# Decode attention and a small FFN on one core: FFN and output projection by column tiles, one product for the softmax denominators, unused matmuls in a loop

## The chip, the cores and the metric

The kernel runs on one core of one Trainium2 chip. The metric is device time in microseconds (us) of one execution, and several executions are compared by their median.

## What is computed

Two tokens (a batch of 2, one query each, width 512) pass a layer norm. The result feeds an attention block with a cache of 8192 keys and values for each of 32 heads of 128, and beside it a two-layer FFN of width 1792 with a ReLU. Both results are added to the input:

```python
xn = _layernorm(x)
q = (xn @ wq) by heads                       # 2 x 32 heads x 128
p = softmax(q . k_cache * 128 ** -0.5)       # over 8192 keys
o = p . v_cache
out = x + o.reshape(2, 4096) @ wo + relu(xn @ w1) @ w2
```

All inputs and the output are bf16. The key and value caches are 128 MiB each; wq and wo are 4 MiB each, w1 and w2 1.75 MiB each. Each byte is read once.

## The kernel before, in words

**The loop.** There are 64 pairs of batch and head. A turn of the loop takes U = 4 of them, so there are NP = 16 turns. Partition p of the tile `ks` (8 MiB) holds 256 keys of one pair, 32 partitions to a pair; `vs` holds the values in the same way. There is one buffer each for keys and for values. In a turn TensorE transposes the 256 key blocks (line 275), while VectorE and ScalarE copy the results to the 32 tiles `kT` (line 429). TensorE then multiplies them with the queries into the PSUM tile `Sc` (line 282). VectorE takes maxima (476, 483), ScalarE takes exponentials (550), adding up each pair's sum into `RS`, one partition slice to a pair, and TensorE multiplies the weights with the values (335). At the end of a turn, in all but the last two, TensorE does `WARM` = 24 products of the identity with itself into `ms`, which nobody reads (346).

**Loads.** All large loads stand in SyncE's queue in program order (lines 182 to 196). The keys of turn t+1 are issued when the transposes of turn t are done, the values of turn t+1 when the value products of turn t are done. After the transposes of the last turn, SyncE issues w1, w2 and then wo in four pieces of 18, 8, 4 and 2 of its 32 rows j (`cuts`, line 153; a row is 128 partitions by 512 columns). They go into `ks`, in front of the output store that waits for `osb`.

**After the loop**, in TensorE's order: four fp32 products of `RS` with `onesh`, one to a pair slot, give the denominators in `Sc` (line 356); four products put x into the eight columns `fin` of `Sc` (362); 56 products of w1 blocks with the two columns of xn give the hidden layer in `ms` (373). Meanwhile VectorE turns denominators and value sums into the normalised output `OTn` (494 to 512), and takes the ReLU to `hT` (516). TensorE transposes `OTn` (385) and regroups it with four products by `sel` (389), and VectorE makes `OX` of it (522). Then come 56 products with w2 and 128 with wo (line 400, in `project`). In these the weights are the stationary operand, 128x128 each, and the two tokens the moving one, two columns wide. All add into `fin`. Before each piece of wo TensorE waits for its load. Last come a copy to `yT` (526), a transpose (420), a copy to `osb` (528) and the store (196).

GpSimd sets up the identity, `sel`, `onesh` and zeros (213 to 230), and in the loop copies the queries of a turn (236).

Of the kernel before, what the change touches and what calls it, by code (L numbers as in the profile page):

```python
# [15 lines left out]
LAG = 32  # L16
TR = (21, 25)
BC = 32
WARM = 24
ON_ACT = (0, 3, 5)  # L20


# [1 line left out]
def kernel(  # L24
# [35 lines left out]
    QG = H * Dh // 512  # L60
    QH = 512 // Dh
    Z = (QG - 1) * Bsz

    inv_sqrt = float(Dh) ** -0.5
    eps = 1e-5
# [9 lines left out]
    def sem(name):  # L75
        return tc.alloc_semaphore(name)
# [10 lines left out]
    kT = [sb([P, EG, P], bf16, f"kT{i}") for i in range(NG)]  # L87
    identb = sb([P, P], bf16, "identb")
    sel = sb([H, DQ, P], bf16, "sel")
    onesh = sb([P, U, P], f32, "onesh")  # L90
    onesb = sb([1, P], bf16, "onesb")
    eps_t = sb([P, 1], f32, "eps_t")
    xsb = sb([Bsz, D], bf16, "xsb")
# [3 lines left out]
    rinv = sb([Bsz, 1], f32, "rinv")  # L97
    xn = sb([Bsz, KT, P], bf16, "xn")

    xz = sb([P, KT, 2 * Z + Bsz], bf16, "xz")  # L100
    qs = sb([QG * Bsz, 512], bf16, "qs")
    qb = sb([P, N], bf16, "qb")
    q4 = sb([P, U], bf16, "q4")
# [2 lines left out]
    mcol = sb([P, 2], bf16, "mcol")  # L106
    mx = sb([1, 2, U], bf16, "mx")
    nm = sb([P, 2, U], f32, "nm")
    RS = sb([P, 2, NP], f32, "RS")
    NM = sb([P, 2, N], f32, "NM")  # L110
    OTf = sb([P, 2, N], f32, "OTf")
    lo = sb([P, N], f32, "lo")
# [6 lines left out]
    OG = sb([P, 2, N], f32, "OG")  # L119
    OTn = sb([P, Bsz, H], bf16, "OTn")  # L120
    Ob = sb([H, Bsz, Dh], bf16, "Ob")
    OX = sb([P, WJ, Bsz], bf16, "OX")
    hT = sb([P, FJ, Bsz], bf16, "hT")
    yT = sb([P, Bsz, KT], bf16, "yT")
    osb = sb([Bsz * KT, P], bf16, "osb")

# [23 lines left out]
    K_all = A_k_cache.rearrange("b h (m kk) d -> (b h m) (kk d)", kk=KB)  # L150
    V_all = A_v_cache.rearrange("b h (m kk) d -> (b h m) (kk d)", kk=KB)
    wo_v = A_wo.rearrange("(p j) n -> p j n", j=WJ)
    cuts = (0, 18, 26, 30, WJ)
    NC = len(cuts) - 1

    KSPLIT = (0, NP - 1)
    VSPLIT = (1, NP - 1)
    NL = 16 * NP
    piece = [(dX, 32), (dQ, 32)] + [(sem(f"dWo{c}"), 16) for c in range(2, NC)]
    qp = ot[0:QG * Bsz, :]  # L160
    tpq = ms[:, 0:N // 2].bitcast(bf16).rearrange("p (l c) -> p l c", l=QH)
    tpx = tp[0][:].rearrange("p g k -> p (g k)")[:, 0:KT * Bsz].rearrange(
        "p (kt b) -> p kt b", b=Bsz
    )
    hp = ms[:, 128:128 + FJ * Bsz].rearrange("p (j b) -> p j b", b=Bsz)
    ox = ms[:, 256:256 + Bsz * WJ]
    fin = Sc[:, 512:512 + KT * Bsz]

# [42 lines left out]
    @(lambda f: f(nc.gpsimd))  # L211
    def _(g):
        g.memset(identb[:], 0.0).then_inc(sG, 1)
        g.memset(sel[:], 0.0).then_inc(sG, 1)
        g.memset(onesh[:], 0.0).then_inc(sG, 1)
        g.wait_ge(sG, 1)
        g.affine_select(
            out=identb[:], in_=identb[:], compare_op=ALU.not_equal, fill=1.0,
            base=0, pattern=[[-1, P]], channel_multiplier=1,
        ).then_inc(sI, 1)  # L220
        g.wait_ge(sG, 2)
        g.affine_select(
            out=sel[:], in_=sel[:], compare_op=ALU.not_equal, fill=1.0,
            base=0, pattern=[[-1, DQ], [1, P]], channel_multiplier=-DQ,
        ).then_inc(sI, 1)
        g.wait_ge(sI, 2)
        g.memset(prm[:], 0.0).then_inc(sG, 1)
        g.wait_ge(sG, 4)
        for u in range(U):
            g.memset(onesh[u * HP:(u + 1) * HP, u, :], 1.0).then_inc(sI, 1)  # L230
            g.wait_ge(sI, 3 + u)
        g.wait_ge(sV, 100)
        for t in range(NP):
            if t > 0:
                g.wait_ge(sS, 2 * t)
            g.tensor_copy(q4[:], qb[:, U * t:U * t + U]).then_inc(sQ1, 1)  # L236
            for d, split in ((dK, KSPLIT), (dV, VSPLIT)):
                if t not in split:
                    g.wait_ge(d[0], 16 * (t + 1)).then_inc(d[1], 16)
        g.wait_ge(dO, 16).then_inc(sG, 1)  # L240


    @(lambda f: f(nc.tensor))
    def _(pe):
# [53 lines left out]
        def spread(i):  # L298
# [2 lines left out]
                bc[:, i, :], lhsT=onesb[:], rhs=mx[:, i, :], start=True, stop=True  # L301
            ).then_inc(sB, 1)

        regs = counters(pe, mybir.EngineType.PE)
        reg, g, h = regs[0], regs[1:3], regs[3:]
        with pe.Fori(16, NL + 1, 16) as n16:
# [35 lines left out]
                if first == KB // 2 - 1:  # L342
                    t.then_inc(sW, 1)
            with pe.If_lt(reg, NP - 1):
                for i in range(WARM):
                    pe.matmul(  # L346
                        ms[:], lhsT=identb[:],
                        rhs=identb[:].rearrange("p (o k) -> p o k", o=1).to_broadcast([P, 4, P]),
                        start=True, stop=True,
                    )  # L350
            advance(pe, regs)

        pe.wait_ge(sI, 2 + U)
        dbp = Sc[:, 0:2 * N].rearrange("p (t u) -> p t u", u=U)
        for u in range(U):
            t = pe.matmul(
                dbp[:, :, u], lhsT=onesh[:, u, :], rhs=RS[:].rearrange("p i t -> p (i t)"),
                start=True, stop=True,
            )
        t.then_inc(sH, 1)  # L360
        for k in range(KT):
            pe.matmul(
                fin[:, k * Bsz:(k + 1) * Bsz],
                lhsT=xsb[:, k * P:(k + 1) * P],
                rhs=identb[0:Bsz, 0:Bsz],
                start=(k == 0),
                stop=False,
            )
        pe.wait_ge(dW1, 16)
        w1_v = w1_sb.rearrange("p kt (f j) -> p kt j f", j=FJ)  # L370
        for j in range(FJ):
            for kt in range(KT):
                i = pe.matmul(
                    hp[:, j, :],
                    lhsT=w1_v[:, kt, j, :],
                    rhs=xz[:, kt, Z:Z + Bsz],
                    start=(kt == 0),
                    stop=(kt == KT - 1),
                )
        i.then_inc(sF, 1)  # L380

        pe.wait_ge(sV, 108)
        tO = tp[0][0:H, 0:Bsz, :]
        for b in range(Bsz):
# [10 lines left out]
            )  # L395
        t.then_inc(sH, 1)

        def project(w, j, x, last=False):
            for k in range(KT):
                t = pe.matmul(  # L400
                    fin[:, k * Bsz:(k + 1) * Bsz],
                    lhsT=w[:, j, k * P:(k + 1) * P],
                    rhs=x[:, j, :],
                    start=False,
                    stop=(last and k == KT - 1),
                )
            return t

        pe.wait_ge(sF, 2)
        pe.wait_ge(dW2, 16)  # L410
        for j in range(FJ):
            project(w2_sb, j, hT)
        pe.wait_ge(sV, 110)
        for c in range(NC):
            pe.wait_ge(*piece[c])
            for j in range(cuts[c], cuts[c + 1]):
                t = project(wo_sb, j, OX, j == WJ - 1)
        t.then_inc(sH, 1)
        pe.wait_ge(sV, 111)
        pe.transpose(  # L420
            tp[1][0:Bsz * KT, 0, :], yT[:].rearrange("p b c -> p (b c)"), identb[:]
        ).then_inc(sH, 1)

    def kcopies(eng, act, h):
# [8 lines left out]
    def _(v):  # L433
        v.memset(eps_t[:], eps).then_inc(sV, 1)
        v.memset(onesb[:], 1.0)
        v.memset(xz[:], 0.0).then_inc(sZ, 1)
        v.wait_ge(dX, 16)
        v.bn_stats(out=stats[:], in_=xsb[:]).then_inc(sV, 1)
        v.wait_ge(sV, 2)
# [50 lines left out]
        def both(ap):  # L490
# [21 lines left out]
        v.tensor_tensor(  # L512
            out=OTn[:].rearrange("p b h -> p (b h)"), in0=OG[:, 0, :], in1=OG[:, 1, :], op=ALU.add
        ).then_inc(sV, 1)
        v.wait_ge(sF, 1)
        v.tensor_scalar(
            out=hT[:], in0=hp, scalar1=0.0, scalar2=None, op0=ALU.max,
        ).then_inc(sF, 1)
        v.wait_ge(sH, 2)
        v.tensor_copy(Ob[:], tp[0][0:H, 0:Bsz, :]).then_inc(sV, 1)  # L520
        v.wait_ge(sH, 3)
        v.tensor_copy(
            OX[:], ox.rearrange("p (b j) -> p j b", b=Bsz)
        ).then_inc(sV, 1)
        v.wait_ge(sH, 4)
        v.tensor_copy(yT[:], fin.rearrange("p (c b) -> p b c", c=KT)).then_inc(sV, 1)
        v.wait_ge(sH, 5)
        v.tensor_copy(osb[:], tp[1][0:Bsz * KT, 0, :]).then_inc(sE, 1)


    @(lambda f: f(nc.scalar))
    def _(a):
        a.wait_ge(sV, 3)
        a.activation(
            out=rstd[:], in_=mv[:, 1:2], func=ACTF.Sqrt, bias=eps_t[:Bsz], scale=1.0
        ).then_inc(sA, 1)

        a.copy(nm[:, 0, 0:1], eps_t[:]).then_inc(sO, 1)
        regs = counters(a, mybir.EngineType.Activation)
        reg, g, h = regs[0], regs[1:3], regs[3:]  # L540
        with a.Fori(0, NP) as t:
            kcopies(a, True, h)
            for i in range(2):
                a.wait_ge(sB, g[i])
                a.copy(nm[:, i, :], bc[:, i, :]).then_inc(sN, 1)  # L545
                a.wait_ge(sN, g[i])
                for u in range(U):
                    own = slice(u * HP, (u + 1) * HP)
                    k = slice(i * KB // 2, (i + 1) * KB // 2)
                    x = a.activation(  # L550
                        out=prm[own, k, u],
                        in_=S[own, k, u],
                        func=ACTF.Exp,
                        bias=nm[own, i, u:u + 1],
                        scale=1.0,
                        accum_out=RS[own, i, bass.ds(t, 1)],
                    )
                x.then_inc(sP, 1)
            a.copy(NM[:, :, bass.ds(t * U, U)], nm[:]).then_inc(sC, 1)
            a.wait_ge(sW, g[1])  # L560
            a.copy(OTf[:, :, bass.ds(t * U, U)], oh[:, :, 0:U]).then_inc(sO, 1)  # L561
            advance(a, regs)
        a.wait_ge(sV, 102)
        a.activation(out=F[:], in_=df[:], func=ACTF.Exp, scale=1.0).then_inc(sA, 1)
# [1 line left out]
_INS = ['A_x', 'A_k_cache', 'A_v_cache', 'A_wq', 'A_wo', 'B_x', 'B_w1', 'B_w2']  # L566
_OUTS = [((2, 1, 512), 'bfloat16')]
# [25 lines left out]
```

## Time and profile before

| What | Value |
|---|---|
| Median of 6 runs | 659.55 us (658.26 to 662.0) |
| Profiled execution, device time | 659.12 us |
| Its span, first to last instruction | 657.3 us |
| Mean granted TensorE clock | 0.967 |
| Read from HBM | 280.50 MB, 427 GB/s over the span |
| Loop's last value product ends | 642.61 us into the span |
| Output store issued | 654.88 us into the span |

The profile counts times from the start of the span. For each engine it tells when instructions ran, what it waited for, and which instruction or load ended the wait. PE is TensorE's products, PEld its loads of stationary operands, DVE is VectorE, ACT is ScalarE, POOL is GpSimd, SP is SyncE. SPq is an engine's queue issuing. A DMA row in a chain is the time from a load's issue to its landing. PEclk is the clock that TensorE was granted, as a share of full speed.

### The profile page before, as it was taken

The numbers are of one execution on the slowest core, as the hardware profiler recorded it, in microseconds if no ns is written. First come the engines' busy times: TensorE is split into PE (matmuls) and PEld (weight loads), VectorE is DVE, ScalarE is ACT, GpSimd is POOL, SyncE is SP. The second block draws the span as 40 slices with busy tenths as digits, with TensorE's granted clock in tenths as the row PEclk, the third lists the DMA queues.
The fourth block names the chain that finished last, engine by engine and source line by source line (L and its number), as shares of the span: only waits on it lengthen the run. The fifth ranks groups of instructions, "written<-read, shape, count | busy, mean of one in ns | idle before, by whom it ended". The sixth has DMA issues, their size and how long they took to land.

```text
span 657.3 us, 27600 instructions
## 1 busy us (share of the span) xinstructions
PE 600.3 (91%) x12987; PEld 544.7 (83%) x12987; DVE 261.9 (40%) x503; ACT 290.8 (44%) x532; POOL 7.1 (1%) x30
## 2 busy tenths in 40 slices
PE   2786999999999999999999999998999999999997
PEld 0586887978889798888979878896987879798987
DVE  1440450716235071632507154260715417072721
ACT  1332443636345263543537354343725435372730
POOL 2000000000000000000000000000000000000000
PEclk9986999999899899999989999999999999899997
DMA  9999999999999999999999999999999999999997
GB/s 379 448 441 437 396 423 443 423 443 419 435 443 431 439 415 423 447 447 431 423 427 443 447 431 423 423 447 443 435 411 435 447 443 431 411 439 427 429 421 290
DMA packets 6223, 280.66 MB, mean 427 GB/s; under 512 B 706, under 2 KB 708, under 8 KB 964
## 3 DMA queue, kind: packets, MB, share of 16 engines
q1 hardware_dynamic: 6208, 280.50, 99.0%
q8 instruction: 8, 0.13, 0.1%
q14 instruction: 3, 0.02, 0.0%
q10 hardware_dynamic: 4, 0.00, 0.0%
HBM read 280.50 MB, written 0.00 MB: 427 GB/s over the span
## 4 chain that ended last, share of the span: by engine, by line
PE 61%; DMA 35%; DVE 1%; issue 1%; SPq 0%; ACT 0%; ACTq 0%
PE tp L275 34%; DMA ks<-in_A_k_cache_dram 31%; PE ot L335 11%; PE Sc L282 10%; PE ms L346 6%; DMA ks<-in_A_wo_dram 4%; DVE mcol L476 1%; PE ms L294 0%; PE ms L300 0%; SPq L194 0%; ACT L429 0%; ACT kT L429 0%; SPq L191 0%; SPq L182 0%; SPq L170 0%
## 5 line engine op out<-in xcount | busy, mean ns | idle before, releaser
L429 DVE COPY kT<-tp 128x1024 bf16<-128x1024 bf16 x320 | 209.3, 688 | 248.8 <-PE tp L275 243.2
L275 PEld LDWEIGHTS tp<-identb,ks 128*128 128x128 bf16 x4096 | 230.6, 98 | 18.3 <-DMA ks<-in_A_k_cache_dram 16.4
L275 PE MATMUL tp<-identb,ks 128*128 128x128 bf16 x4096 | 233.1, 220 | 12.6 <-DMA ks<-in_A_k_cache_dram 11.7
L429 ACT COPY kT<-tp 128x1024 bf16<-128x1024 bf16 x192 | 188.1, 1014 | 122.7 <-PE tp L275 122.7
L335 PE MATMUL ot<-prm,vs 128*128 128x64 bf16 x4096 | 139.2, 197 | 1.6 <-issue 1.6
L335 PEld LDWEIGHTS ot<-prm,vs 128*128 128x128 bf16 x4096 | 135.1, 100 | 3.5 <-issue 1.7
L282 PE MATMUL Sc<-q,kT 128*128 128x64 bf16 (+8 forms) x4096 | 134.2, 192 | 3.2 <-issue 3.1
L282 PEld LDWEIGHTS Sc<-q,kT 128*128 128x128 bf16 x4096 | 129.6, 98 | 4.7 <-issue 3.4
L346 PE MATMUL ms<-identb 128*128 128x512 bf16 x336 | 74.8, 379 | 0.0
L476 DVE TENSOR_REDUCE mcol<-Sc 32x1 bf16<-32x128 f32 x128 | 37.1, 290 | 93.6 <-PE Sc L282 92.3
L550 ACT ACTIVATE prm<-Sc,nm 32x128 bf16<-32x128 f32 x128 | 69.0, 539 | 5.4
L545 ACT COPY nm<-ms 128x4 f32<-128x4 f32 x32 | 5.2, 163 | 142.1 <-PE ms L300 142.1
L346 PEld LDWEIGHTS ms<-identb 128*128 128x128 bf16 x336 | 31.8, 97 | 36.4
L561 ACT COPY OTf<-ot 128x8 f32 x16 | 2.7, 166 | 76.2 <-PE ot L335 76.2
L550 ACT ACTIVATION_READ_ACCUMULATOR prm<-Sc,nm x128 | 32.1, 251 | 0.0
L294 PE MATMUL ms<-identb,mcol 128*1 128x128 bf16 x32 | 7.0, 218 | 22.1 <-DVE mcol L476 22.1
L294 PEld LDWEIGHTS ms<-identb,mcol 128*1 128x1 bf16 x32 | 2.5, 79 | 23.9 <-issue 23.1
L429 ACT ACT_TABLE_LOAD x16 | 20.5, 1283 | 3.6 <-issue 3.5
L254 PE MATMUL ot<-vs,xz 128*16 128x512 bf16 x32 | 8.5, 431 | 8.7 <-DMA vs<-in_A_wq_dram 8.7
L483 DVE TENSOR_REDUCE mx<-ms 1x4 bf16<-1x128 bf16 x32 | 8.9, 279 | 13.8 <-PE ms L294 13.8
L254 PEld LDWEIGHTS ot<-vs,xz 128*16 128x16 bf16 x32 | 3.1, 98 | 13.7 <-issue 10.8
L236 POOL COPY q<-qb 128x4 bf16<-128x4 bf16 x16 | 3.0, 188 | 591.6 <-PE Sc L282 573.2
(61 smaller groups left out, 47.5 us busy)
## 6 DMA issues: line engine op xcount, KB each, us to landing
ks<-in_A_k_cache_dram SPq DMA_DIRECT2D x4, 4096.0 KB, 23.0
vs<-in_A_v_cache_dram SPq DMA_DIRECT2D x4, 4096.0 KB, 21.8
vs<-in_A_wq_dram SPq DMA_DIRECT2D x1, 4096.0 KB, 12.2
ks<-in_B_w_dram SPq DMA_DIRECT2D x2, 1792.0 KB, 16.5
ks<-in_A_wo_dram SPq DMA_DIRECT2D x1, 2304.0 KB
ks<-in_A_wo_dram SPq DMA_DIRECT2D x1, 1024.0 KB, 25.7
ks<-in_A_wo_dram SPq DMA_DIRECT2D x1, 512.0 KB, 26.4
ks<-in_A_wo_dram SPq DMA_DIRECT2D x1, 256.0 KB, 26.6
```

What stands on the lines that cost most here:

```text
L236: g.tensor_copy(q4[:], qb[:, U * t:U * t + U]).then_inc(sQ1, 1)
L254: i = pe.matmul(qp, lhsT=xz[:, kt, Z - g * Bsz:Z - g * Bsz + QG * Bsz], rhs=vs[:, (kt * QG + g) * 512:(kt * QG + g + 1) * 512], start=(g = ...
L275: t = pe.transpose(tp[e % 4][:, i, :], ks[:, kk * Dh:(kk + 1) * Dh], identb[:])
L282: t = pe.matmul(Sc[:, U * kk:U * (kk + n)], lhsT=kT[e][:, i, :], rhs=rep(q4[:], n), start=True, stop=True,)
L294: pe.transpose(trp[:, i * P:(i + 1) * P], mcol[:, i:i + 1], identb[:]).then_inc(sT, 1)
L335: t = pe.matmul(oh[:, i, :], lhsT=vs[:, kk * Dh:(kk + 1) * Dh], rhs=rep(prm[:, kk, :], REP), start=(first == 0), stop=(first == KB // 2 - 1),)
L346: pe.matmul(ms[:], lhsT=identb[:], rhs=identb[:].rearrange("p (o k) -> p o k", o=1).to_broadcast([P, 4, P]), start=True, stop=True,)
L429: fn(kT[e][:], tp[e % 4][:]).then_inc(kR[e % HG], 1)
L476: m = v.tensor_reduce(out=mcol[own, i:i + 1], in_=S[own, i * KB // 2:(i + 1) * KB // 2, u], axis=AX.X, op=ALU.max,)
L483: v.tensor_reduce(out=mx[:, i, :], in_=trp[:, i * P:(i + 1) * P].rearrange("o (u m) -> o u m", u=U), axis=AX.X, op=ALU.max, negate=True,). ...
L545: a.copy(nm[:, i, :], bc[:, i, :]).then_inc(sN, 1)
L550: x = a.activation(out=prm[own, k, u], in_=S[own, k, u], func=ACTF.Exp, bias=nm[own, i, u:u + 1], scale=1.0, accum_out=RS[own, i, bass.ds( ...
```

## The change

- **Unused matmuls.** The 24 products at the end of a turn become 25, written as a loop of five turns with five products in its body.
- **Denominators.** `RS` gets a column for each of the four pair slots (128 columns in place of 32) and is zeroed at the start by GpSimd. One fp32 product with a 128x128 tile of ones replaces the four.
- **Hidden layer.** Operands are swapped: the activations, padded to CT = 32 columns, are stationary, and w1 is the moving operand, 448 contiguous columns at a time. Four products of a `kt` write to PSUM partitions 0, 32, 64 and 96 onward (16 products in all). ScalarE copies the result to `hb`, 14 small products turn it round into `hq`, and VectorE takes the ReLU in four instructions.
- **w2 and 22 rows of wo.** The same swap: one product of 32 stationary columns by 512 moving ones a row, with the output partitions cycling over 0, 32, 64 and 96 of a tile `y`. VectorE copies `y` to `ys`, and four fp32 products with `sel2` add the four partition groups into `fin`. x is added to `y` by one product.
- **The last 10 rows of wo** stay as before, in `fin`. wo comes in five pieces of 14, 8, 4, 4 and 2 rows.
- GpSimd zeroes `OX`, now 32 columns a row in the place of `kT2`, after the last scores, and `hT` at the start. VectorE makes `sel2` at the start.

```diff
+    cuts = (0, 14, 22, 26, 30, WJ)
+    WIDE = 2
 # TensorE
+        def warm(n):
+            with pe.Fori(0, n):
+                for i in range(5):
+                    pe.matmul(ms[:], lhsT=identb[:], rhs=identb[:]....to_broadcast([P, 4, P]), ...)
...
-                for i in range(WARM):
-                    pe.matmul(ms[:], lhsT=identb[:], ...)
+                warm(5)
...
-        for u in range(U):
-            t = pe.matmul(dbp[:, :, u], lhsT=onesh[:, u, :], rhs=RS...)
+        pe.matmul(Sc[:, 0:2 * N], lhsT=ones[:], rhs=RS[:]...., start=True, stop=True).then_inc(sH, 1)
...
+        for kt in range(KT):
+            for c in range(TC):
+                i = pe.matmul(
+                    tile(hp, c)[:, 0:FJ * CT],
+                    lhsT=xz[:, kt, Z:Z + CT],
+                    rhs=w1_sb[:, kt, c * FJ * CT:(c + 1) * FJ * CT], ...)
+        i.then_inc(sF, 1)
+        pe.matmul(tile(y, 0), lhsT=identb[0:Bsz, 0:CT], rhs=xsb[:], start=True, stop=False)
+        pe.wait_ge(sF, 2)
+        for j in range(FJ):
+            t = pe.matmul(hq[...], lhsT=hb[:, j, :], rhs=rows, start=True, stop=True)
+        t.then_inc(sF, 1)
...
+        pe.wait_ge(sF, 4)
         pe.wait_ge(dW2, 16)
         for j in range(FJ):
-            project(w2_sb, j, hT)
+            c = j % TC
+            pe.matmul(tile(y, c), lhsT=hT[:, j, :], rhs=w2_sb[:, j, :], ...)
         pe.wait_ge(sV, 110)
+        for i in range(WIDE):
+            pe.wait_ge(*piece[i])
+            for j in range(cuts[i], cuts[i + 1]):
+                t = pe.matmul(tile(y, j % TC), lhsT=OX[:, j, :], rhs=wo_sb[:, j, :], ...)
+        t.then_inc(sH, 1)
+        for i in range(WIDE, NC):
+            if i == WIDE:
+                pe.wait_ge(sF, 5)
+                for k in range(KT):
+                    pe.matmul(fin[...], lhsT=ys[:, k * P:(k + 1) * P], rhs=sel2[:], ...)
+            pe.wait_ge(*piece[i])
+            for j in range(cuts[i], cuts[i + 1]):
+                for k in range(KT):
+                    t = pe.matmul(fin[...], lhsT=wo_sb[:, j, k * P:(k + 1) * P], rhs=OX[:, j, 0:Bsz], ...)
 # VectorE
-        v.tensor_scalar(out=hT[:], in0=hp, scalar1=0.0, scalar2=None, op0=ALU.max)
+        v.wait_ge(sF, 3)
+        for c in range(TC):
+            m = v.tensor_scalar(out=hT[c * CT:(c + 1) * CT, :, 0:Bsz], in0=hq..., ..., op0=ALU.max)
...
+        v.wait_ge(sI, 3)
         v.tensor_copy(OX[:, :, 0:Bsz], ox...)
         v.wait_ge(sH, 4)
+        v.tensor_copy(ys, y).then_inc(sF, 1)
 # ScalarE
-                        accum_out=RS[own, i, bass.ds(t, 1)],
+                        accum_out=RS[own, i, bass.ds(t, 1), u],
...
+        a.wait_ge(sF, 1)
+        a.copy(hb, hp[:, 0:FJ * CT].rearrange("p (f j) -> p j f", j=FJ)).then_inc(sF, 1)
 # GpSimd
+        g.wait_ge(sS, 2 * NP)
+        g.memset(OX, 0.0).then_inc(sI, 1)
```

## The prediction

> **What bounds the kernel now.** I read the page from the top, since the slices and the queues tell whether any engine can be the bound at all.
>
> ```profile
> span 657.3 us, 27600 instructions
> ...
> PEclk9986999999899899999989999999999999899997
> DMA  9999999999999999999999999999999999999997
> ...
> q1 hardware_dynamic: 6208, 280.50, 99.0%
> q8 instruction: 8, 0.13, 0.1%
> ```
>
> The DMA row is at 9 in every slice but the last, and one queue alone takes 99.0% of the 16 engines' time. Does TensorE, 91% busy, hold the loads up? The waits of TensorE between 75 and 600 us, in which 13 turns start, answer that:
>
> ```profile
> PE ms L294 <- DVE mcol L476: 18.0, 13, 1.4
> PE tp L275 <- DMA ks<-in_A_k_cache_dram: 7.9, 7, 1.3
> ```
>
> Seven of those turns start with TensorE waiting for keys, 7.9 us in all. So TensorE is not the bound, but nearly: 7.9 / 13 = 0.6 us a turn. In the chain of waits the keys of turns 2, 3, 6, 9 and 11 land at 112.35, 151.03, 267.14, 383.26 and 460.66 us: 38.70 us a turn throughout, 16.78 MB at 433 GB/s. From 112.35 to the last landing at 653.66 there are 234.3 MB, 540.6 us at that rate; 541.3 pass. The loads run almost without a gap to the end.
>
> Then the end, first by the chain, in order of time (start, us, what):
>
> ```profile
> 627.07 26.60 DMA ks<-in_A_wo_dram
> 653.66 0.05 issue
> 653.71 0.38 PE Sc L400 x8
> 654.09 0.02 issue
> 654.12 0.18 DVE yT L526
> 654.29 0.04 issue
> 654.34 0.28 PE tp L420
> ```
>
> The chain waits for the last 2 rows of wo; only 8 products follow, then copy, transpose, copy and store. All of this stays. What the change can move is whether TensorE is ready at 653.66. The timeline (start, us, engine, line) gives its work before:
>
> ```profile
> 642.56 1.07 PE L356 MATMUL Sc<-RS,onesh 128*128 128x32 f32 x8
> ...
> 643.75 3.52 PE L373 MATMUL ms<-xz,ks 128*128 128x2 bf16 x56
> ...
> 648.18 1.65 PE L400 MATMUL Sc<-hT,ks 128*128 128x2 bf16 x56
> ...
> 649.69 3.17 PE L400 MATMUL Sc<-OX,ks 128*128 128x2 bf16 x104
> ```
>
> TensorE waits in front of the second, third and fourth piece of wo: it is just ahead of the loads.
>
> **The change, part by part.** All times are those of the profiled execution (659.12 us, span 657.3), 0.43 below the median of the runs, 659.55.
>
> *When wo lands.* The trace has the waits end at 651.84 (row 26), 653.07 (row 30) and 653.66 (row 32). A row is 0.131 MB, 0.30 us. So row 22 lands near 650.6 and row 14 near 648.2. The bytes are the same; the fifth piece costs SyncE one issue more (0.43 us, the row of the wo issues), 26 us before the landing, so I cost it at nothing. If it delayed the stream, it would be by that 0.43.
>
> *Loop of five.* A product takes 5.18 / 24 = 0.216 us (line 346), so the 25th costs 0.22 us a turn, 3.0 over 14 turns. It is covered by the waits for keys (7.9 us). The branches: before shows the outer loop's jump back once without unused products in front of it, between turns 14 and 15: "609.36 1.96 PE L275 ... [0.17 <-issue]". So a jump costs at most 0.17 us where nothing covers it. Here five products of 1.08 us stand ahead of each jump. Bounds: 0 to 5 x 0.17 = 0.85 us a turn. I take 0, as at the outer jump of the other turns, where the transposes follow the unused products without a gap (184.90 + 5.18 = 190.08 us in the chain).
>
> [...]
>
> *Denominators.* Eight passes of 32 columns took 1.07 us; two passes of 128 columns take 0.27 (a quarter of the passes) to 1.07 (the same columns). I take 0.5. `DF` then waits for ScalarE's exponentials instead, which end at 643.01 + 0.31 = 643.32: 0.35 earlier than before. `OTn` is ready at 645.55, not 645.87.
>
> *Hidden layer.* 448 columns cost 448/512 x 0.216 = 0.19 us, 16 products 0.76 us if the four partition groups run at once and 3.0 one after another, against 3.52. At once: 643.05 to 643.8. ScalarE's copy of 448 columns, between its 0.166 for 8 and 1.014 for 1024, is 0.53: 644.4. The 14 products cost between 29 and 63 ns each (lines 400 and 373), 0.4 to 0.9, so `hq` is ready near 645.0, ahead of `OTn`. In front of `Ob`, VectorE now has four ReLU instructions of 0.19 in place of one: 0.76, to 646.35. `Ob` 0.28, regroup 0.39, `OX` 0.23 and hand-offs: `OX` near 647.4, before it was 648.51. The GpSimd zeroing of `OX` (0.95 us for 128x1024, the row of `prm`) starts with the last maxima at 633.0; if it held VectorE up, all this would come up to 0.95 later. I take 0.
>
> *w2 and 22 rows of wo.* Nothing in the trace shows four partition groups at once. The nearest row, line 254 (16 stationary, 512 moving columns, always the same partitions), took 8.49 / 32 = 0.265 us a product. So a row costs 0.216 / 4 = 0.054 to 0.265. The granted clock matters too: it fell from 1.00 to 0.54 at 647.5 and 0.50 later, in the windows of 2.5 us. I take four at once, because nothing in the operands or outputs ties the groups together, and reckon with both clocks:
>
> | Step, ends at | clock 1.0 | clock 0.5 |
> |---|---|---|
> | w2, 4 rounds, from 647.1 | 648.0 | 648.8 |
> | rows 0 to 14, 3.5 rounds, landed 648.2 | 649.0 | 650.4 |
> | rows 14 to 22, 2 rounds, landed 650.6 | 651.1 | 651.5 |
> | `ys` copy 128x512 | 651.9 | 652.3 |
> | four fp32 products, 8 passes | 652.9 | 653.3 |
> | rows 22 to 26, 16 products of 0.03 | 653.4 | 653.8 |
> | rows 26 to 30, landed 653.07 | 653.9 | 654.3 |
> | rows 30 to 32, landed 653.66, 0.38 | 654.2 | 654.6 |
>
> The `ys` copy is 0.68 (line 458, 16x512, fp32) and 0.1 of hand-off; the passes 1.0 by line 356, and 0.3 if they go like the narrow products of line 400. Before ended at 654.09. So the end comes 0.1 to 0.5 later; with 2.0 for the fp32 passes at half clock 1.5 later, with 0.3 as early as before, since the last 8 products still wait for 653.66. I take +0.5. It cannot come earlier.
>
> [...]
>
> **Rivals.**
> 1. *The column groups run one after another* (slower). For: the row of line 254. Against: different stationary operands and different output partitions, products free of each other. `hq` is 2.3 later, `OX` near 649.1; w2 then takes 14 x 0.216 = 3.0, to 651.9, the 22 rows 4.75, to 656.6, `ys` 657.4, the fp32 products 658.4, the 40 narrow ones 659.7: 5.6 us after 654.09. Total 659.55 + 5.6 = 665.2; at half clock another 7.8. It decides as soon as a row costs over about 0.10 us.
> 2. *The small loop's jumps are exposed* (slower). 14 x (0.85 + 0.22) = 15.0 us more on TensorE, less 7.9 of waits. A further 2.8 or so is taken up because keys are issued ahead: 24.2 us from issue to landing, less 19.35 of transfer and about 2 of fixed delay (the output store: 654.88 to the end, 2.4). That leaves 4.3: 663.9. It decides from (7.9 + 2.8 - 3.0) / 70 = 0.11 us a jump on. Against: nothing showed at the outer jump of 14 turns.
> 3. *Faster.* TensorE's tail is shorter by more than a microsecond before `OX`, and the program is smaller. But 653.66 is set by bytes, and what follows it is unchanged. At most the 0.7 us that the span from 112.35 on might hold over the steady rate would go, plus less of the slow first turn: 658.5.
>
> **The numbers.** Forecast: no change beyond what can be told, 659.55 + 0.5 = 660.0; chance 0.80. Rival 1: 0.08. Rival 2: 0.06. Rival 3 by over 0.3%: 0.03. Something unforeseen and slower: 0.03. A measurement of this kernel can tell about 0.3% (2 us) from no change, so: faster 0.03, same 0.80, slower 0.17. Range 658.6 to 662.5: from rival 3 to the forecast with 1.5 for the passes, 0.95 for the zeroing and 0.5 for what the runs differ. Rivals 1 and 2 are left out, with 0.14 between them.
>
> **What would show it.** After: the last wo load still lands near 653.7 in the span and the 8 products follow at once; a wait of TensorE for keys still starts several turns; 25 products in 5.4 us. Column groups at once: the 14 and 22 wide products end in about 0.9 and 1.2 us of work at full clock, and not 3.0 and 4.75. The forecast fails if the landing itself moves, which I have no reason for, or if TensorE comes to rows 30 to 32 later than 654.5.

## The result, and the profile after

Over 24 executions the changed kernel has a median of 660.97 us (659.56 to 664.76), against 659.33 for before (50 executions beside it). The ratio is 1.0027 (95% interval 1.0019 to 1.0036): 1.8 us slower by the ratio, just under the 2 us that the prediction calls no change, and the interval doesn't reach 1. The profiled execution of after took 664.43 us with a span of 662.6. It is near the slowest of the 24, so its span says less about the typical loss than its steps do.

The page of after, the lines that answer to those of before:

```profile
span 662.6 us, 27519 instructions
...
PEclk9996898999999899999999999999999999999988
DMA  9999999999999999999999999999999999999996
...
q1 hardware_dynamic: 6352, 280.50, 98.8%
q8 instruction: 7, 0.11, 0.1%
```

The picture is the same: the same 280.50 MB, every slice but the last at 9. The clock rows differ in a few slices; the one that matters here is the fifth (66 to 82 us), 8 where before has 9: TensorE ran slower there for a while. The waits of TensorE between 75 and 600 us (line, what for, us in total, times, longest):

```profile
PE tp L288 <- DMA ks<-in_A_k_cache_dram: 13.0, 11, 1.7
```

TensorE waits for keys more than before (13.0 us against 7.9), although it does more work. So it isn't TensorE that became the bound: the keys come later. The chain shows one turn's start, and the end (start, us, what); the first two lines and the rest are from two windows of the same view:

```profile
226.47 5.40 PE ms L320 x25
231.86 14.31 PE tp L288 x256
```

```profile
632.18 26.42 DMA ks<-in_A_wo_dram
...
658.65 0.39 PE Sc L448 x8
...
659.06 0.18 DVE yT L576
```

The 25 unused products take 5.40 us, 0.216 each, and the transposes follow at once: no jump shows. At the end the 8 products still follow the last landing, but the landing is at 658.60, not 653.66. That is 4.94 of the 5.3 us by which this execution is longer. TensorE's own tail, from the timeline (start, us, engine, line; idle before in brackets):

```profile
648.70 0.48 PE L370 MATMUL Sc<-RS,ones 128*128 128x128 f32 x2
649.11 0.94 PE L381 MATMUL tp<-ks,xz 128*32 128x448 bf16 x16
...
652.84 1.04 PE L421 MATMUL tp<-ks,hT 128*32 128x512 bf16 x14
653.51 1.24 PE L429 MATMUL tp<-ks,kT 128*32 128x512 bf16 x14
655.07 0.62 PE L429 MATMUL tp<-ks,kT 128*32 128x512 bf16 x8 [0.33 <-DMA ks<-in_A_wo_dram]
656.49 1.05 PE L438 MATMUL Sc<-sel,kT 128*128 128x2 f32 x8 [0.80 <-DVE kT L574]
...
658.65 0.37 PE L448 MATMUL Sc<-kT,ks 128*128 128x2 bf16 x8 [0.26 <-DMA ks<-in_A_wo_dram]
```

Here the granted clock was 1.00 from 643.8 to 657.4, and TensorE was ready when the last load landed.

*Where the loads lost time.* The landings in the trace show the gap. In after's profile the keys of turn 2 land at 114.34, 22.17 us after the second half of the values of turn 1 (92.17); in before's it is 20.13 us (112.35 and 92.22). A steady step is 19.35 us for 8.39 MB. So 2.82 us against 0.78 are lost there. Several later landings of after lose 0.1 to 0.67 more, some 2.7 us together, and these two parts make up most of the 4.94. The cause stands in SyncE's queue, between 85 and 95 us, first of before, then of after:

```profile
88.03 0.33 SPq L182 DMA_DIRECT2D ks<-in_A_k_cache_dram  x1
```

```profile
89.84 0.33 SPq L194 DMA_DIRECT2D ks<-in_A_k_cache_dram  x1
```

The keys were asked for 1.81 us later and came 1.99 later. TensorE was late by then: the value products of turn 0 ended at 69.77 instead of 68.52, at clock 0.50 between 66.9 and 70.4. Is that the change, or this one execution? The experiments had to tell.

*What comes after the last landing.* From the last landing to the end of the span it is 4.02 us, before 3.67. The 8 products, copy, transpose, copy and store take the same. The difference, 0.35, lies at the very end: GpSimd waits for the store, and the step from that wait to its next instruction takes 0.455 us (661.051 to 661.506) against 0.101 in before (656.112 to 656.213). These are events of the trace that the page leaves out.

### The profile page after: what moved, and what is told of

Its sections match the earlier page's. It is cut to its first block, busy times and chain, and to the rows that moved or that the text cites. A ratio compares the mean times of both kernels' runs of the same rounds, so it can differ in the third digit from the quotient of the medians.

```text
span 662.6 us, 27519 instructions
## 1 busy us (share of the span) xinstructions
PE 598.0 (90%) x12866; PEld 535.9 (81%) x12866; DVE 263.4 (40%) x508; ACT 291.2 (44%) x533; POOL 7.3 (1%) x29
## 3 DMA queue, kind: packets, MB, share of 16 engines
q1 hardware_dynamic: 6352, 280.50, 98.8%
HBM read 280.50 MB, written 0.00 MB: 423 GB/s over the span
## 4 chain that ended last, share of the span: by engine, by line
DMA 49%; PE 47%; issue 1%; DVE 1%; SPq 1%; ACT 0%; ACTq 0%
DMA ks<-in_A_k_cache_dram 45%; PE tp L288 34%; PE ot L357 6%; PE Sc L295 5%; DMA ks<-in_A_wo_dram 4%; PE ms L320 2%; DVE mcol L519 1%; SPq L206 0%; PE ms L307 0%; ACT L466 0%; ACT kT L466 0%; PE ms L313 0%; SPq L203 0%; SPq L194 0%; SPq L182 0%
## 5 line engine op out<-in xcount | busy, mean ns | idle before, releaser
L357 PE MATMUL ot<-prm,vs 128*128 128x64 bf16 x4096 | 136.0, 195 | 2.0 <-issue 2.0
L357 PEld LDWEIGHTS ot<-prm,vs 128*128 128x128 bf16 x4096 | 132.0, 99 | 3.9 <-issue 2.1
L320 PE MATMUL ms<-identb 128*128 128x512 bf16 x350 | 78.2, 380 | 0.0
L320 PEld LDWEIGHTS ms<-identb 128*128 128x128 bf16 x350 | 33.4, 98 | 38.3 <-issue 0.5
L267 PE MATMUL ot<-vs,xz 128*16 128x512 bf16 x32 | 10.0, 488 | 8.4 <-DMA vs<-in_A_wq_dram 8.4
## 6 DMA issues: line engine op xcount, KB each, us to landing
ks<-in_A_wo_dram SPq DMA_DIRECT2D x1, 1024.0 KB, 24.3
```

The costliest lines, as they stand in the source:

```text
L267: i = pe.matmul(qp, lhsT=xz[:, kt, Z - g * Bsz:Z - g * Bsz + QG * Bsz], rhs=vs[:, (kt * QG + g) * 512:(kt * QG + g + 1) * 512], start=(g = ...
L320: pe.matmul(ms[:], lhsT=identb[:], rhs=identb[:].rearrange("p (o k) -> p o k", o=1).to_broadcast([P, 4, P]), start=True, stop=True,)
L357: t = pe.matmul(oh[:, i, :], lhsT=vs[:, kk * Dh:(kk + 1) * Dh], rhs=rep(prm[:, kk, :], REP), start=(first == 0), stop=(first == KB // 2 - 1),)
```

## The experiments

Theories at this point: (1) the loads' gap in the early turns, by the loop or by something else in the change (A, and E2 for the keys of turn 2, in the expectations); (2) the new tail costs the time (B), because TensorE comes late to the last rows of wo when the clock is at half (D); (3) GpSimd's last step (F). C and E are the rivals stated with them. Each ratio below is to before, run on the same chip beside the kernel, and isn't the quotient of two medians of the table: the medians of before were 659.62 us beside the e runs, 659.45 beside the f runs and 659.38 beside the g runs. One execution of e6 (2045.06 us) and one of before beside the e runs (1487.52 us) lie far out and don't count in the ratios. "After the landing" is the time from the last landing of wo to the end of the span in the profiled execution.

| Kernel | Median us | Ratio (95%) | After the landing |
|---|---|---|---|
| before | 659.33 | 1 | 3.67 |
| after | 660.97 | 1.0027 (1.0019 to 1.0036) | 4.02 |
| e1_loop_only | 659.90 | 1.0004 (0.9990 to 1.0018) | 3.68 |
| e2_tail_only | 660.72 | 1.0024 (1.0009 to 1.0039) | 5.30 |
| e3_25_straight | 659.88 | 1.0007 (0.9988 to 1.0026) | 3.68 |
| e6_after_ksplit | 660.88 | 1.0005 (0.9984 to 1.0025) | 4.91 |
| f1_wide_one_piece | 660.25 | 1.0010 (0.9997 to 1.0023) | 4.60 |
| f2_bf16_sum | 660.36 | 1.0012 (1.0001 to 1.0023) | 3.95 |
| f3_fill_tail | 659.97 | 1.0015 (1.0003 to 1.0028) | 4.01 |
| f4_wide_one_bf16 | 659.69 | 0.9999 (0.9982 to 1.0017) | 4.03 |
| g1_one_more_gpsimd | 659.70 | 1.0002 (0.9992 to 1.0012) | 3.65 |
| g2_split_keys2 | 660.41 | 1.0020 (0.9996 to 1.0043) | 3.65 |
| g3_before_split_keys2 | 659.48 | 1.0001 (0.9979 to 1.0022) | 3.68 |
| g4_before_one_less_gpsimd | 659.34 | 1.0003 (0.9993 to 1.0014) | 4.06 |

### The loop alone, and everything but the loop

e1_loop_only is before with the loop of five by five in place of the 24 products:

```diff
-                for i in range(WARM):
-                    pe.matmul(ms[:], lhsT=identb[:], ...)
+                with pe.Fori(0, 5):
+                    for i in range(5):
+                        pe.matmul(ms[:], lhsT=identb[:], ...)
```

> The kernel before with the unused products as a loop of five turns of five (25), all else as before. Theory A (the loads' queue runs dry in the first turns because the transposes of turn 1 end later, the tail costs nothing): slower than before by about as much as the change, 1.0 to 2.5 us, with the keys of turn 2 landing near 114 us and not 112.4. Theory B (the new tail costs the time): within 0.5 us of before. Theory C (neither: the executions differ by chance in the early turns): within 0.7 us of before.

e2_tail_only is after with 24 products written out in place of the loop:

```diff
-                warm(5)
+                for i in range(24):
+                    pe.matmul(ms[:], lhsT=identb[:], ...)
```

> The changed kernel with 24 unused products written out, as before: the new tail, denominators and set-up alone. Theory A: within 0.5 us of before. Theory B: slower than before by 1.5 to 2.0 us, with a longer way from the last landing of wo to the store than the 1.2 us of before. Theory C: within 0.7 us of before.

e3_25_straight is before with 25 products written out:

```diff
+WARM = 25
```

> The kernel before with 25 unused products in place of 24, written out. If the extra 0.22 us a turn is what matters (theory A, by the 25th product): slower than before by 0.2 to 1.0 us. If the jumps or the moved program matter (theory A, by the loop): within 0.3 us of before. Theory B: within 0.3 us of before.

Measured: 1.0004 for the loop alone, 1.0007 for 25 straight, 1.0024 for all but the loop. The loop costs nothing that can be told, and neither does the 25th product; the loss goes with the tail and the set-up. The intervals of e1 and e2 overlap, so this comparison points there and doesn't prove it. In the profiles of e1 and e2 the keys of turn 2 came without any gap, so neither part alone brings the early gap (one execution each). What e2's profile does show is the tail. Its chain, the last part:

```profile
625.24 24.63 DMA ks<-in_A_wo_dram
...
649.92 1.07 PE tp L434 x8
...
651.01 0.70 DVE kT L579
...
651.76 1.87 PE Sc L443 x8
653.63 1.08 PE Sc L453 x40
```

The chain no longer ends at the last landing. It hangs on the second piece of wo (landed 649.87), and goes from there through TensorE and VectorE to the end. The last landing was at 653.01, the last of the 40 narrow products ended at 654.71. Had TensorE been ready, they would have ended 0.43 after the landing as in before (654.09 against 653.66), at 653.4: 1.3 us lost. The windows of 2.5 us of e2 tell why (PE, PEld, DVE, ACT, POOL busy and counts, then the granted clock, DMA share, GB/s):

```profile
645.00:647.50 2.50, 1.29 (x18) 0.50 (x18) 0.76 (x4) 0.00 (x0) 0.00 (x0) 0.85 0.98 383
647.50:650.00 2.50, 1.97 (x18) 0.61 (x22) 0.00 (x0) 0.00 (x0) 0.00 (x0) 0.50 0.98 400
650.00:652.50 2.50, 1.70 (x12) 0.80 (x12) 0.69 (x1) 0.00 (x0) 0.00 (x0) 0.50 0.67 261
```

The clock falls to 0.50 from 646.7. At half clock the 8 fp32 passes take 1.87 us in place of 1.05, the rows 14 to 22 take 1.05 in place of 0.62. In before the clock falls at about the same time (0.50 from 647.7):

```profile
645.00:647.50 2.50, 2.48 (x40) 2.29 (x39) 0.84 (x4) 0.00 (x0) 0.00 (x0) 1.00 0.97 411
647.50:650.00 2.50, 2.15 (x72) 2.06 (x73) 0.50 (x2) 0.00 (x0) 0.00 (x0) 0.54 0.96 390
```

But there nearly all that is left are the products of two columns with w2 and wo, and they take about 0.03 us each at either clock (56 in 1.65 us here at 0.50; f3 below has 40 in 1.18 us, nearly all at 1.00). So the new tail is exposed to the clock, and the old one is not.

### Keys in halves in every turn

e6_after_ksplit issues the keys of every turn in two halves, the first after half of the transposes:

```diff
-    KSPLIT = (0, NP - 1)
+    KSPLIT = tuple(range(NP))
```

> The changed kernel with the keys of every turn loaded in two halves, the first issued when the first half of the transposes is done. Theory A: the queue no longer runs dry behind the values, so the landings follow each other at 19.35 us from the first turns on; 1.5 to 3.0 us faster than the change, at or up to 1 us below before. Theory B: no faster than the change by more than 0.5 us.

Measured: the landings have no gap from turn 1 on, as they should, but the median stays at 660.88. Its profile has the tail of e2: last landing 653.94, products ended 655.63, and 2.4 us outside the span where after has 1.8. The median is 1.3 us over that of before beside it, the ratio 1.0005 (0.9984 to 1.0025): they point different ways, so it decides nothing about time.

### Shortening the tail behind the wide products

f1_wide_one_piece gives only the first piece of wo (14 rows) to the wide products, so the fp32 step comes one piece earlier:

```diff
-    WIDE = 2
+    WIDE = 1
```

> The changed kernel with only the first piece of wo (14 rows) in wide products; rows 14 to 32 are narrow as before. Theory D (TensorE's clock halves after the loop, and the late steps of the new tail, the copy of y and the four fp32 products, then end after the last landing): the copy and the fp32 products now stand ahead of rows 14 to 22, so TensorE is ready at the last landing at either clock; the last 8 products start within 0.2 us of the landing, and the time is within 0.5 us of before, about 1.3 us under the change. Theory E (the difference comes from the loads of the first turns alone): as the change, 1 to 2 us over before.

f2_bf16_sum sums the groups in bf16 (the four groups' sums are rounded to bf16 ahead of the last addition):

```diff
-    sel2 = sb([P, Bsz], f32, "sel2")
+    sel2 = sb([P, Bsz], bf16, "sel2")
...
-    ys = kT[1][:].rearrange("p g k -> p (g k)").bitcast(f32)
+    ys = kT[1][:].rearrange("p g k -> p (g k)")[:, 0:D]
```

> The changed kernel with the copy of y and the 0/1 operand in bf16, so that the four products that add the partition groups take one pass each (the sums of the groups are rounded to bf16 ahead of the last sum). Theory D: the four products take about 0.3 us in place of 1.05 or 1.87, TensorE is ready at or within 0.3 us of the last landing, and the time is within 0.6 us of before. Theory E: as the change.

f3_fill_tail keeps after's work and puts 16 unused 128x512 products (into `ot`) into TensorE's gaps after the loop:

```diff
+        def fill(n):
+            for i in range(n):
+                pe.matmul(ot[:], lhsT=identb[:], ...)
...
+        fill(3)
         pe.wait_ge(sV, 110)
         for i in range(WIDE):
+            if i > 0:
+                fill(4)
             pe.wait_ge(*piece[i])
...
+                fill(3)
                 pe.wait_ge(sF, 5)
```

> The changed kernel with 16 unused 512-column products in TensorE's gaps between the loop and the fp32 products, so that the clock has no reason to fall. Theory D: the granted clock stays 1.00 up to 652 us or later, the fp32 products take about 1.05 and not 1.87 us, and the time is within 0.6 us of before. If the clock falls all the same, or the time stays 1 to 2 us over before with the clock at 1.00, theory D is wrong in that step.

f4_wide_one_bf16 is f1 and f2 together.

> Both the first and the second kernel of this call: one wide piece and bf16 sums. Theory D: no faster than either, within 0.5 us of before, since the last landing sets the end. A gain of over 0.7 us on before would say that the tail before was not hidden either.

Measured: f1 1.0010, f2 1.0012, f3 1.0015, f4 0.9999. The two cures together take away the whole loss: the interval of f4 (0.9982 to 1.0017) lies just below that of after (1.0019 to 1.0036), each against before on its own chip, and g1 below, with the same two cures, is at 1.0002. Each alone leaves some 0.7 us, more than the 0.5 and 0.6 that were expected, with intervals too wide to split it finely. f2's profile has the four products at 0.25 us, as expected:

```profile
655.04 0.25 PE L438 MATMUL Sc<-sel,kT 128*128 128x2 bf16 x4 [0.79 <-DVE kT L575]
...
655.98 0.82 PE L448 MATMUL Sc<-kT,ks 128*128 128x2 bf16 x24 [0.29 <-DMA ks<-in_A_wo_dram]
```

The last landing is at 656.40 and the products end 0.41 later, so in that execution the tail wasn't late at all. Its clock was at half from 650.5 to 653.9 and full behind that, up to 657.3. In f1's profile the tail is still late, which its expectation didn't have:

```profile
652.60 1.87 PE L438 MATMUL Sc<-sel,kT 128*128 128x2 f32 x8 [0.78 <-DVE kT L574]
654.33 2.06 PE L448 MATMUL Sc<-kT,ks 128*128 128x2 bf16 x72
```

The fp32 step at half clock still takes 1.87, and now 72 narrow products, 2.06 us, are queued behind it; they end at 656.40, 1.01 after the landing at 655.39, and so about 0.6 late. With bf16 as well, f4 has its 24 last products waiting for a landing again (they idle 0.93 us for it), with the clock still at half:

```profile
649.72 0.27 PE L438 MATMUL Sc<-sel,kT 128*128 128x2 bf16 x4 [0.79 <-DVE kT L575]
...
652.73 0.84 PE L448 MATMUL Sc<-kT,ks 128*128 128x2 bf16 x24 [0.93 <-DMA ks<-in_A_wo_dram]
```

f3 tests the clock itself. Its windows:

```profile
645.00:647.50 2.50, 2.50 (x24) 0.80 (x22) 0.68 (x3) 0.00 (x0) 0.00 (x0) 1.00 0.99 400
...
650.00:652.50 2.50, 2.46 (x30) 1.42 (x29) 0.69 (x1) 0.00 (x0) 0.00 (x0) 1.00 0.65 256
```

```profile
651.32 1.05 PE L454 MATMUL Sc<-sel,kT 128*128 128x2 f32 x8
652.23 1.18 PE L464 MATMUL Sc<-kT,ks 128*128 128x2 bf16 x40
```

With TensorE kept busy the clock stays at 1.00 to 653.1, the fp32 step takes 1.05, and the products end at 653.43, 0.43 after the landing at 653.00, as in before. So useless products, by keeping the clock, are worth 1.3 us in the profile, against e2. The median gains less than that over after (about 0.8 by the ratios, with intervals that overlap). By its ratio f3 is still 1.0 us over before (0.5 by the medians), with the clock at 1.00: the expectation had named 1 to 2 us as the sign that theory D is wrong in that step, and f3 stands at its edge. Of the 1.0, 0.35 is GpSimd's step; the rest, and some 0.4 of f2's 0.8, isn't explained by a late tail in the profiles and lies within the intervals.

### GpSimd's last step

The step of 0.46 us came in after, e2 and f1 to f4, whose traces have 77 GpSimd instructions; kernels with 78 (before, e1, e3) have 0.10, and so has e6 with 63. Theory F: it goes with where the program ends. g1_one_more_gpsimd adds one unused memset (and its tile `pad`) to f4:

```diff
         g.memset(RS[:], 0.0).then_inc(sG, 1)
+        g.memset(pad[:, 0:1], 0.0)
```

> One wide piece and bf16 sums, with one more GpSimd instruction at the start (a memset of an unused word), so that GpSimd's program has as many instructions as before. Theory F (the 0.36 us that every run with the new set-up shows between the store's landing and the last instruction come from where GpSimd's last jump lies in its program): GpSimd's step after the store's wait takes 0.10 and not 0.46 us, the span ends about 3.65 us after the last landing and not 4.0, and the time is within 0.5 us of before. Rival: the pause belongs to the zeroing of the operand ahead of that wait, and stays at 0.46.

g4_before_one_less_gpsimd takes one away from before (VectorE does it instead):

```diff
-        g.memset(onesh[:], 0.0).then_inc(sG, 1)
...
-        g.wait_ge(sG, 4)
+        g.wait_ge(sZ, 2)
...
+        v.memset(onesh[:], 0.0).then_inc(sZ, 1)
```

> The kernel before with one GpSimd instruction less (the zeroing of the tile for the denominators is done by VectorE at the start), all else the same. Theory F: GpSimd's step after the store's wait takes 0.46 us in place of 0.10, and the span ends 4.0 us after the last landing and not 3.64. Rival: it stays at 0.10.

Measured: in g1 the step is 0.10 and 3.65 us lie after the landing; in g4 it is 0.46, and 4.06. An instruction more takes the step away, one less brings it on, whichever kernel it is; why one instruction makes that difference isn't shown. The price, 0.35 us of 659, is visible in the traces only: the medians (1.0002 for g1, 0.9999 for f4; 1.0003 for g4) can't tell it from nothing.

### Keys of turn 2 in halves

g2_split_keys2 is g1 with the keys of turn 2 issued in halves, and an unused memset more; g3_before_split_keys2 is the same on before:

```diff
-    KSPLIT = (0, NP - 1)
+    KSPLIT = (0, 2, NP - 1)
```

> As the kernel before it in this call, and the keys of turn 2 loaded in two halves, the first issued when half of turn 1's transposes are done. Theory E2 (a part of the spread in all kernels is the queue running dry ahead of the keys of turn 2): no gap over 0.2 us between the landings of turn 1's values and turn 2's keys, fewer executions over 661 us, median 0.3 to 1.0 us under before. Rival: the gaps come from the memory and not from a late issue; median within 0.3 us of before.

> The kernel before with the keys of turn 2 in two halves (GpSimd's program kept at the same length). Theory E2: as in the kernel before it in this call, median 0.3 to 1.0 us under before; if both gain alike, the tail of the change is worth nothing once its late steps are cut. Rival: within 0.3 us of before.

Measured: 1.0020 (0.9996 to 1.0043) and 1.0001 (0.9979 to 1.0022). In g2's profile the gap at turn 2 is gone (0.59 is lost at the values behind it), yet no time is won in either kernel. The expected gain isn't there. g2 has both cures of f4 as well, and its 8 executions, with an interval from before to past after, can't tell it from either. Nor does the gap belong to one of the kernels: in the profiles it was 0.78 us in before, 2.82 in after, none in e1, e2, f3, f4 and g4, 0.21 in e3, 1.42 in f1, 2.32 in f2 and 1.24 in g1. The three largest gaps are in the profiles where the clock was at half up to 70 us or later (after, f1, f2), and e1, at half up to 66.7, has none; that is one execution each, not a test. f4 is level with before, with the same loop as after. What makes single executions 2 to 4 us longer stays open: after has 9 of 24 over 661.5 us and before 2 of 50 beside it, but before itself has 6 of 34 beside the e runs.

No version is measurably faster than before; f4 and g1 equal it.

## Why the prediction was right, and where it was off

The forecast was 660.0 with "no change beyond what can be told"; 660.97 was measured, within the range and within the 0.3%. The direction and the place, TensorE's late arrival at the end, were right; the size was not, and that "no change" held owes something to luck: the 1.8 us stand close to the 2 us that count as none, and the interval (to 1.0036) goes past it.

- **What bounds the kernel.** Right. The last products end 0.41 to 0.44 us after the last landing in the profiles of before, after, f2, f3, f4 and g1. Most of TensorE's shorter tail is therefore worth nothing: in e2 the w2 products begin at 645.85, before at 648.18, and TensorE then waits 0.70 us for wo.
- **Loop of five: 0.22 us a turn, hidden, jumps 0.** Right: 5.40 us a turn and nothing behind it (in the chain of after the 25 products start at 226.47 and the transposes at 231.86); e1 1.0004. Rival 2 fell. The queue q8, "instruction" on the page, has 7 packets in after and 8 in before.
- **Denominators, hidden layer.** Predicted 0.5, 0.76, 0.53 (ScalarE's copy), 0.4 to 0.9 (14 products) and 0.76 (ReLUs); measured 0.48, 0.94, 0.53, 0.51 and 0.74. Right, but for 0.18 on the w1 products.
- **Column groups at once.** Right: 14 products of 512 columns in 1.04 us, and 14 x 0.216 = 3.0 one after another. Rival 1 fell. 14 x 0.054 would have been 0.76. One product of 512 columns alone took 0.39 us in after (0.216 in a stream), and three rounds of 0.216 with a last one of 0.39 make the 1.04. So four groups were worth a factor of 3.0 / 1.04 = 2.9 here, and not 4.
- **Nothing on GpSimd beyond the zeroing of `OX`.** That zeroing was hidden, as taken. But its program is one instruction shorter, and its last step 0.35 longer (0.455 against 0.101): a term that the sum did not have, as it took all that follows the landing as unchanged.
- **TensorE comes 0.5 later to the end.** This is the step that was off: "rows 30 to 32" at 654.6 in the half-clock column, with the fp32 products taken at 1.0 at either clock. They take 1.05 at full and 1.87 at half clock; the bound ("with 2.0 for the fp32 passes at half clock 1.5 later") had it, and the value taken did not. e2 shows 1.3 us lost against its own landing and f1 0.6; after's profiled execution and f3, both at full clock, show none. The choice of 1.0 leaned on line 356, measured at a clock of 1.00, for a step that the prediction itself put after the clock's fall at 647.5.
- **"It cannot come earlier"**: nothing faster than before was measured. Two signs were named that the forecast fails, and both are met in a profile. "If the landing itself moves, which I have no reason for": in after's it moved by 4.94 us; the experiments don't tie that to the change. "If TensorE comes to rows 30 to 32 later than 654.5", 0.84 after their landing: in e2's it came to them about 1.5 us after the landing.

Together: of the 1.8 us, 0.35 is GpSimd's step, shown by g1 and g4; between nothing and 1.3 is the late tail, by the clock of the execution, shown by e2 and f3, and taken back by f4 and g1. The fastest executions fit that: 659.56 us in after and 659.55 in e2, 658.44 in f4 and 658.58 in g1, 658.00 to 658.56 in before. Only one execution of each kernel was profiled, so how often the half clock meets the tail isn't known, and the two don't make an exact sum.

## What to carry to other kernels

A shorter chain of compute ahead of a last load was worth nothing here, since the load lands later anyway, and it can cost: TensorE lost its clock in the tail of both kernels (0.50 from 647.7 us in before, from 657.4 in after), and the 8 fp32 passes left behind the last waits took 1.87 us in place of 1.05 in e2. What stands behind the last waits should be work that a low clock doesn't slow, which here is narrow bf16 products (0.03 us each at either clock) rather than wide or fp32 ones, or the last big step should come a piece earlier. Price each step of a tail with a row taken at the clock that it will have.

## What the runs showed of the hardware

- **A low clock slows products unequally.** At 0.50 against 1.00, 8 fp32 passes of 2 columns took 1.87 against 1.05 us, 14 wide bf16 products 1.89 against 1.04; bf16 products of 2 columns with w2 and wo took 0.03 each at either.
- **Busy time in the profile doesn't tell when the clock falls.** In the traces of before and after, each stretch at half clock that ends within the span lasted 3.41 us, but for one of 10.24, three times that, in each (50.38 to 60.62 and 49.87 to 60.11). In the 3.41 us ahead of the fall in the tail TensorE was busy for 1.94 us in e2 (643.32 to 646.73) and 2.30 in after (654.03 to 657.45), but 3.18 in before (644.30 to 647.71) and all 3.41 in e3 (640.98 to 644.39); and 3.41 us with 2.19 busy in after (650.62 to 654.03) were followed by as long a stretch at 1.00. With the gaps filled by products of 512 columns the clock stayed at 1.00 up to 653.1 in f3. What makes it fall isn't shown.
- **One GpSimd instruction more or less showed at the end of the span.** With 78 or 77 of them in the trace, the step from GpSimd's wait for the store to its next instruction took 0.10 or 0.46 us, and 3.65 us (g1) or 4.06 (g4) lay after the last landing.
- **Keys asked for 1.81 us later landed 1.99 later** (turn 2, after against before), although the load took 24.3 us from issue to landing in before and a load passes in 19.35 in steady flow. In that turn before already had a gap of 0.78, so nothing was left in reserve; the prediction had reckoned with 2.8 us.
